# The corners of TensorE taken diagonally, and a gate on GpSimd taken away, in a linear-attention and SiLU feed-forward kernel

## The chip, the cores and the metric

The kernel runs on one core of a Trainium2 chip. A core has five engines, each with its own queue of instructions that it takes in order: TensorE (PE in the profile; its weight loads are PEld), VectorE (DVE), ScalarE (ACT), GpSimd (POOL) and SyncE (SP), which here only issues transfers. The engines wait for each other through semaphores. The metric is the device time of one execution in microseconds (us), the median of several runs.

## The reference: what is computed

q, k and v have 8 batches, 8 heads, 576 positions and 64 features in float32. For each batch and head:

```
q_s = softmax of q over its 64 features
k_s = softmax of k over the 576 positions
kv  = k_s^T v                (64 x 64)
attn = q_s kv                (576 x 64)
x = attn, heads side by side (4608 tokens x 512)
h = x w_in                   (4608 x 2048)
out = (h * sigmoid(h)) w_out (4608 x 512)
```

## The kernel before

**Tiling.** The 4608 tokens are taken in 9 chunks of 512 (`TCH`), the attention in 8 batches of 576. For each chunk t the kernel forms x, multiplies by w_in (the "group" products, `group`, line 374), applies SiLU, and multiplies by w_out (`prod`, line 474). Both large products are done by a scheme with seven block products in place of eight (products 1 to 7, taken in the order 1, 2, 6, 5, 7, 4, 3). It needs sums and differences of blocks as operands. For the second product these are S1, S2, S3 and S4, made by `s_op` on VectorE from the SiLU's output: S2 is made from S1, S4 from S2. Product 5 reads S1, product 6 reads S2, product 7 what S3 wrote, product 3 reads S4.

**Attention.** Two heads share the 128 partitions in places: TensorE's array of 128 x 128 is used as four corners of 64 x 64. A corner has a row half (the 64 partitions of its operands) and a column half (the 64 partitions of its output). `kv(b, cc)` (line 195) makes k^T v of four heads with 9 steps j of four products each, one for every corner, with 65 columns (64 of v and one that sums k's weights). There r is the row half and PS's bank, s the column half. `xt_mm` (line 234) makes x^T: four products, one for each corner, with s the row half and the bank and r the column half. `vaug` is the bfloat16 copy of v with the extra column, made by `vcast`, in two halves cc = 0 and 1, on GpSimd for batches 2 to 7. `qnorm` (GpSimd, line 163) multiplies exp(q) by the reciprocal of its sum, which VectorE makes (lines 154 and 158). `q_transpose` (SyncE) then transposes it by a transfer.

**Order.** The program is written out by hand. A list `units` holds TensorE's work in units of eight products, from chunk 1 on alternately of chunk t's group products and of chunk t-1's second products (`four_pairs`). `plan(u, f)` puts other work in front of unit u; whatever it issues goes into the queue of its engine at that place of the program. `full(t)` plans chunks 2 to 6. There u is the chunk's first unit and b = t + 1 the batch whose attention is prepared. Every queue runs in its own order, and an instruction starts as soon as its semaphores allow.

**Around the change.** For chunk 2 alone the second half of batch 3's v is treated differently. Batch 3's loads are issued late, by SyncE in front of the group products of chunk 1's last third (q 0, k 1, k 0, v 0, v 1, q 1, in this order). `vcast_at` puts in front of that cast a copy of one element of S2 into the tile `gate` on GpSimd. GpSimd, which works in order, so starts the cast only when S2 has been made. It is planned at unit 6 of chunk 2, S1 at unit 4 and S2 at unit 5. The PS banks that matter: a chunk's group products 5, 3 and 2 are gathered in banks 2 and 3, and `group_add` (line 352, VectorE) reads them, so that TensorE's next product 2 or 5 must wait for that addition. In the last chunk S1 and S2 are made in two halves: `plan(begin[NCH] - 11, ...)` gives S1's second half.

Of the kernel before, what the change touches and what calls it, by code (L numbers as in the profile page):

```python
# [17 lines left out]
def kernel(  # L18
# [9 lines left out]
    nc = tc.nc  # L28
# [12 lines left out]
    NCH = NT // TCH  # L41
# [21 lines left out]
    SS = {i: glob.tile([128, HF, HT], FP16, name=f"S{i}") for i in (1, 2, 4)}  # L63
# [8 lines left out]
    gate = glob.tile([1, 1], FP32, name="gate")  # L72
# [14 lines left out]
    def copy(eng, o, i):  # L87
        if eng is nc.scalar:
            eng.copy(out=o, in_=i)  # L89
        else:  # L90
            eng.tensor_copy(o, i)  # L91
# [7 lines left out]
    def jgd(b, name, cc):  # L99
        return st[b][name, cc].rearrange("p g (j d) -> p j g d", d=D)  # L100
# [4 lines left out]
    def exp_q(b, cc, g0=0, g1=2):  # L105
        if "eq" not in st[b]:
            st[b]["eq"] = ap.tile([128, J, NG * D], BF16, name="eq")
        nc.scalar.activation(  # L108
            out=half(st[b]["eq"], cc)[:, :, g0:g1], in_=jgd(b, "qt", cc)[:, :, g0:g1], func=ACT.Exp
        )  # L110

    def exp_k(b, cc):
        nc.scalar.activation(out=half(ek, cc), in_=jgd(b, "kt", cc), func=ACT.Exp)  # L113

    def vcast(b, cc, eng, g0=0, g1=2):
        o = vaug[:, :, 2 * cc + g0:2 * cc + g1, 0:D]
        i = jgd(b, "vt", cc)[:, :, g0:g1, :]
        copy(eng, o, i)

    def vcast_at(t, b, cc):  # L120

        if t == 2 and cc == 1:
            nc.gpsimd.tensor_copy(gate, SS[2][0:1, 0, 0:1])
        vcast(b, cc, nc.gpsimd)

    def qsum_pair(b, cc):
        e = half(st[b]["eq"], cc)
        t1 = mp.tile([128, 2 * TCH], FP32, name="h0", bufs=1)[:, 0:J * D]
        t1 = t1.rearrange("p (j g d) -> p j g d", g=2, d=D // 2)
        t2 = mp.tile([128, 2 * TCH], FP32, name=f"h{cc + 1}", bufs=1)[:, 0:J * D // 2]  # L130
        t2 = t2.rearrange("p (j g d) -> p j g d", g=2, d=D // 4)
        nc.gpsimd.tensor_tensor(  # L132
            out=t1, in0=e[:, :, :, 0:D // 2], in1=e[:, :, :, D // 2:D], op=ALU.add
        )
        nc.gpsimd.tensor_tensor(
            out=t2, in0=t1[:, :, :, 0:D // 4], in1=t1[:, :, :, D // 4:D // 2], op=ALU.add
        )
        st[b]["t2", cc] = t2
# [51 lines left out]

    def kv(b, cc):
        for j in range(J):
            for r in range(2):
                for s in range(2):
                    nc.tensor.matmul(  # L195
                        out=PS[s * 64:(s + 1) * 64, 6 + r, cc * 128:cc * 128 + E1],
                        lhsT=ek[r * 64:(r + 1) * 64, j, (2 * cc + s) * D:(2 * cc + s + 1) * D],
                        rhs=vaug[r * 64:(r + 1) * 64, j, 2 * cc + s, :],
                        start=(j == 0),
                        stop=(j == J - 1),  # L200
                    )
# [13 lines left out]
    def kv_both(b):  # L215
        kv(b, 0)
        kv(b, 1)
        kvcopy(b)
# [9 lines left out]
        return got  # L228

    def xt_mm(b, cc, col, n, bank, dst):  # L230
        for r in range(2):
            for s in range(2):
                h = slice(s * 64, (s + 1) * 64)
                nc.tensor.matmul(  # L234
                    out=PS[r * 64:(r + 1) * 64, bank + s, dst:dst + n],
                    lhsT=kvn[b % 3][h, cc, r, :],
                    rhs=st[b]["qT"][h, col // P:(col + n) // P, cc, r * 64:(r + 1) * 64],
                )
# [117 lines left out]
    def group_silu(t, i, f, n):  # L356
        x = group_bank(t, False) if i is None else four(t, i)
        nc.scalar.activation(out=group_out(t, f, n), in_=x, func=ACT.Silu, scale=1.0 / XS)  # L358

    def group(t, g, i, on=None, defer=False):  # L360
        bank = 0 if i in (1, 6, 7, 4) else 6 if t == 1 else 2
        w, f0, f1 = WS[g], 4 * g + 8, 4 * g
        a, bb = {
            1: (wa(0, f0), xb(t, 0, 0)),
            2: (wa(1, f0), xb(t, 1, 0)),
            3: (w[3], xb(t, 1, 1)),
            4: (wa(1, f1), XS4[3]),
            5: (w[0], XS4[0]),
            6: (w[1], XS4[1]),
            7: (w[2], XS4[2]),  # L370
        }[i]
        for p in range(4):
            for c in range(2):
                nc.tensor.matmul(  # L374
                    out=PS[:, bank + p // 2, (p % 2) * HT:(p % 2) * HT + width(t)],
                    lhsT=a[:, c, p * 128:(p + 1) * 128],
                    rhs=bb[:, c, 0:width(t)],
                    start=(i in (1, 2, 5) and c == 0 and p % 2 == 0),
                    stop=(i in (2, 3, 4) and c == 1 and p % 2 == 1),
                    skip_group_check=True,  # L380
                )
        on = on or {}
        if i == 1:
            group_snap(t, 0)
        elif i == 2:
            group_add(t, 0)
        elif i == 6:
            group_snap(t, 1, on.get(1, nc.scalar))
        elif i == 7:
            group_snap(t, 2, on.get(2, nc.scalar))  # L390
            group_add(t, 2)
        elif i == 4:
            group_silu(t, None, f1, 0)
        elif i == 3:
            if not defer:
                group_silu(t, 2, f1, 1)
                group_silu(t, 0, f0, 0)
            group_add(t, 1)
# [37 lines left out]
    def blk(t, kh, th):  # L436
        return GTS[t % 2][:, kh * HF:(kh + 1) * HF, th * HT:(th + 1) * HT]

    def s_op(t, i, f0=0, f1=HF):
        in0, in1, op = {  # L440
            1: (blk(t, 0, 1), blk(t, 1, 1), ALU.add),
            2: (SS[1], blk(t, 0, 0), ALU.subtract),
            3: (blk(t, 0, 0), blk(t, 0, 1), ALU.subtract),
            4: (blk(t, 1, 0), SS[2], ALU.subtract),
        }[i]
        f = slice(f0, f1)
        o = blk(t, 0, 1) if i == 3 else SS[i]
        nc.vector.tensor_tensor(out=o[:, f], in0=in0[:, f], in1=in1[:, f], op=op)
# [170 lines left out]
    def plan(u, f):  # L619
        at.setdefault(u, []).append(f)  # L620
# [7 lines left out]
    begin = {1: len(units)}  # L628
# [3 lines left out]
    def b_units(t, order):  # L632
        got = []
        for i in order:
            got.append(lambda t=t, i=i: prod(t, i, 0))

            def second(t=t, i=i):
                prod(t, i, 1)
                after(t, i)

            got.append(second)
        return got
# [11 lines left out]
    def full(t):  # L654
        begin[t] = u = len(units)
        b = t + 1
        bs = b_units(t - 1, ORDER)
        gs = [
            lambda g=g, i=i: group(t, g, i, {1: nc.vector} if g else {2: nc.vector}, True)
            for g in (1, 0)  # L660
            for i in ORDER
        ]
        for x in 2 * four_pairs:
            units.append({"b": bs, "g": gs}[x].pop(0))
        for i, x in ((1, 4), (2, 5), (3, 15), (4, 19)):
            plan(u + x, lambda i=i: s_op(t - 1, i))
        for g, at3 in ((1, (13, 17, 15)), (0, (23, 28, 25))):
            f1, f0 = 4 * g, 4 * g + 8
            for i, x, f, n in zip(range(3), at3, (f0, f0, f1), (0, 1, 1)):
                plan(u + x, lambda i=i, f=f, n=n: group_silu(t, i, f, n))  # L670
        more = b + 1 < B
        for i in range(2):
            plan(u + (3, 10)[i], lambda i=i: exp_q(b, i))
            plan(u + (7, 11)[i], lambda i=i: qsum(b, i))
            plan(u + (16, 17)[i], lambda i=i: qnorm(b, i, nc.gpsimd))
            plan(u + (2, 6 if t == 2 else 11)[i], lambda i=i: vcast_at(t, b, i))
            plan(u + (6, 4)[i], lambda i=i: exp_k(b, i))
            if more:
                plan(u + (5, 12)[i], lambda i=i: load(b + 1, "qt", q, i, nc.sync))
                plan(u + (8, 6)[i], lambda i=i: load(b + 1, "kt", k, i, nc.sync))  # L680
                plan(u + (22, 23)[i], lambda i=i: load(b + 1, "vt", v, i, nc.sync))
        plan(u + 17, lambda: q_transpose(b))
        plan(u + 15, lambda: kv_both(b))
        plan(u + 22, lambda: xt(t + 1, 0, nc.vector))
        plan(u + 27, lambda: xt(t + 1, 1))
        plan(u, lambda: (xs_op(t, 1), xs_op(t, 2), xs_op(t, 3), xs_op(t, 4)))
# [24 lines left out]

    begin[NCH] = len(units)
    last = NCH - 1
    plan(begin[NCH] - 11, lambda: s_op(last, 1, 4, 8))
    plan(begin[NCH] - 7, lambda: s_op(last, 2, 4, 8))
    plan(begin[NCH], lambda: (s_op(last, 1, 0, 4), s_op(last, 2, 0, 4), s_op(last, 3)))
    plan(begin[NCH] + 6, lambda: s_op(last, 4))
# [139 lines left out]
```

## Time and profile before

| what | us |
|---|---|
| median of 3 runs | 262.11 (262.06 to 262.53) |
| the profiled execution | 262.06 |
| its span | 260.3 |
| TensorE busy | 251.4 |
| VectorE busy | 206.8 |
| ScalarE busy | 187.6 |
| GpSimd busy | 66.3 |

The span runs from the first to the last instruction on the core; the profiled execution's own time is 1.8 us longer than its span. The lines quoted below are of two kinds. A line of the timeline gives the start and the length in us, the engine, the line of the kernel, the operation, what it writes and reads (`out<-in`), the shape and how many instructions were merged; in brackets stands how long the engine stood idle before it, and what ended that. TensorE's products are pipelined: the time of a merged group of eight includes the tail of the last, so the distance from one group's start to the next, 0.87 us, is the true pace. The lines on transfers give the time from issue to landing. PS is the memory that TensorE writes, W the weights, GT the SiLU's output, S any of S1, S2 and S4, T the differences of w_out's blocks (T1 to T4), XT and XS x^T and its differences, h the sums between the group products, WS differences of w_in's blocks.

### The profile page before, as it was taken

The numbers are of one execution on the slowest core, as the hardware profiler recorded it, in microseconds if no ns is written. First come the engines' busy times: TensorE is split into PE (matmuls) and PEld (weight loads), VectorE is DVE, ScalarE is ACT, GpSimd is POOL, SyncE is SP. The second block draws the span as 40 slices with busy tenths as digits, with TensorE's granted clock in tenths as the row PEclk, the third lists the DMA queues.
The fourth block names the chain that finished last, engine by engine and source line by source line (L and its number), as shares of the span: only waits on it lengthen the run. The fifth ranks groups of instructions, "written<-read, shape, count | busy, mean of one in ns | idle before, by whom it ended". The sixth has DMA issues, their size and how long they took to land.

```text
span 260.3 us, 6411 instructions
## 1 busy us (share of the span) xinstructions
PE 251.4 (97%) x2732; PEld 203.0 (78%) x2732; DVE 206.8 (79%) x268; ACT 187.6 (72%) x212; POOL 66.3 (25%) x63
## 2 busy tenths in 40 slices
PE   8799999999999999999999999999999999999992
PEld 3357756656888888888888888888888888888881
DVE  2957798888997999799979997999798548855832
ACT  5757887898993899489948994899473848484610
POOL 1753791640351205030502060306000000000003
PEclk9999999999999999999999999999999999999999
DMA  7999999689989485958694869630443004300624
GB/s 256 342 193 299 303 329 331 237 181 390 306 306 254 108 248 189 240 119 223 213 256 107 229 209 193 166 75 3 91 87 77 3 0 88 76 3 1 141 63 121
DMA packets 35452, 45.89 MB, mean 176 GB/s; under 512 B 16208, under 2 KB 19984, under 8 KB 35424
## 3 DMA queue, kind: packets, MB, share of 16 engines
q1 hardware_dynamic: 29568, 33.69, 47.6%
q0 software_dynamic: 5616, 11.60, 16.9%
q8 instruction: 21, 0.34, 0.5%
q10 hardware_dynamic: 240, 0.20, 0.2%
q14 instruction: 7, 0.06, 0.1%
HBM read 36.70 MB, written 9.44 MB: 177 GB/s over the span
## 4 chain that ended last, share of the span: by engine, by line
PE 88%; DVE 4%; ACT 2%; POOL 2%; DMA 1%; issue 1%; POOLq 0%; ACTq 0%
PE PS L474 37%; PE PS L374 35%; PE PS L411 5%; PE PS L264 3%; PE PS L282 2%; PE PS L234 2%; PE PS L195 2%; DMA qt<-in_q_dram 1%; DVE eq L163 1%; DVE zq L154 1%; ACT sg L256 1%; POOL out_dram L736 1%; ACT eq L108 1%; DVE GT L257 1%; POOL h L132 0%
## 5 line engine op out<-in xcount | busy, mean ns | idle before, releaser
L352 DVE TENSOR_TENSOR h<-PS,h 128x1024 f32<-128x1024 f32 (+1 forms) x45 | 54.0, 1199 | 13.0 <-ACT h L89 6.8
L474 PEld LDWEIGHTS <-GT 128*128 128x128 f16 x512 | 49.5, 98 | 6.9 <-issue 1.2
L374 PEld LDWEIGHTS <-WS 128*128 128x128 f16 x480 | 46.8, 98 | 6.4 <-issue 0.4
L474 PE MATMUL PS<-W,GT 128*128 128x256 f16 x384 | 49.1, 273 | 0.0
L374 PE MATMUL PS<-XS,WS 128*128 128x256 f16 (+1 forms) x360 | 46.3, 272 | 0.0
L358 ACT ACTIVATE GT<-h 128x1024 f16<-128x1024 f32 (+1 forms) x45 | 46.1, 1047 | 0.3 <-DVE h L352 0.3
L89 ACT COPY h<-PS 128x1024 f32<-128x1024 f32 (+1 forms) x35 | 35.1, 1003 | 13.4 <-PE PS L374 12.9
L163 POOL TENSOR_TENSOR eq<-eq,rzq 128x1152 bf16<-128x1152 bf16 x13 | 27.7, 2133 | 53.8 <-DVE rzq L158 53.4
L474 PEld LDWEIGHTS <-S 128*128 128x128 f16 x384 | 37.2, 98 | 5.2 <-issue 1.0
L374 PEld LDWEIGHTS <-W 128*128 128x128 f16 x360 | 34.7, 98 | 4.8 <-issue 0.5
L474 PE MATMUL PS<-T,S 128*128 128x256 f16 x256 | 32.7, 273 | 0.0
L374 PE MATMUL PS<-XT,W 128*128 128x256 f16 (+1 forms) x240 | 29.5, 272 | 0.1
L358 ACT ACTIVATE GT<-PS 128x1024 f16<-128x1024 f32 (+1 forms) x15 | 15.2, 1016 | 18.9 <-PE PS L374 18.9
L91 POOL CAST vaug<-vt 128x1152 bf16<-128x1152 f32 x12 | 14.8, 1239 | 43.3 <-DMA vt<-in_v_dram 43.3
L736 POOL DMA_DIRECT2D out_dram<-ow x5 | 2.7, 546 | 72.5 <-DVE ow L721 72.5
L108 ACT ACTIVATE eq<-qt 128x1152 bf16<-128x1152 f32 (+1 forms) x18 | 19.0, 1057 | 2.5 <-DMA qt<-in_q_dram 2.5
L154 DVE TENSOR_REDUCE zq<-eq 128x18 f32<-128x1152 bf16 x12 | 16.1, 1346 | 3.8 <-ACT eq L108 3.8
L113 ACT ACTIVATE ek<-kt 128x1152 bf16<-128x1152 f32 x16 | 18.3, 1153 | 0.8 <-DMA kt<-in_k_dram 0.8
L264 PE MATMUL PS<-XT,W 128*128 128x288 f16 x128 | 16.4, 286 | 0.5 <-DVE XT L91 0.2
L474 PE MATMUL PS<-W,S 128*128 128x256 f16 x128 | 16.5, 273 | 0.0
L494 DVE SCALAR_TENSOR_TENSOR ow<-PS,sc 128x512 f32<-128x512 f32 x7 | 4.8, 692 | 14.5 <-ACT sc L490 14.5
L264 PEld LDWEIGHTS <-W 128*128 128x128 f16 x128 | 12.4, 98 | 4.4 <-issue 1.3
(79 smaller groups left out, 345.4 us busy)
## 6 DMA issues: line engine op xcount, KB each, us to landing
out_dram<-ow SPq DMA_DIRECT2D x64, 128.0 KB, 2.4
qt<-in_q_dram SPq DMA_DIRECT2D x12, 576.0 KB, 4.7
kt<-in_k_dram SPq DMA_DIRECT2D x12, 576.0 KB, 5.7
vt<-in_v_dram SPq DMA_DIRECT2D x12, 576.0 KB, 5.4
qt<-in_q_dram POOLq DMA_DIRECT2D x4, 576.0 KB, 10.5
kt<-in_k_dram POOLq DMA_DIRECT2D x4, 576.0 KB, 13.9
vt<-in_v_dram POOLq DMA_DIRECT2D x4, 576.0 KB, 12.9
W<-in_moe_w_out_dram POOLq DMA_DIRECT2D x4, 512.0 KB, 15.0
```

The lines of the kernel that those rows point to most:

```text
L89: eng.copy(out=o, in_=i)
L91: eng.tensor_copy(o, i)
L108: nc.scalar.activation(out=half(st[b]["eq"], cc)[:, :, g0:g1], in_=jgd(b, "qt", cc)[:, :, g0:g1], func=ACT.Exp)
L113: nc.scalar.activation(out=half(ek, cc), in_=jgd(b, "kt", cc), func=ACT.Exp)
L154: nc.vector.reduce_sum(out=z, in_=e, axis=AX.X)
L163: eng.tensor_tensor(out=e, in0=e, in1=r[:, :, :, None].to_broadcast([128, J, 2, D]), op=ALU.mult)
L264: nc.tensor.matmul(out=PS[:, 2 * (fb % 3) + n, 0:S // 2], lhsT=W1[:, c, fb * 128:(fb + 1) * 128], rhs=XTS[0][:, c, n * (S // 2):(n + 1) * ...
L352: nc.vector.tensor_tensor(out=four(t, i), in0=group_bank(t, True), in1=four(t, i), op=ALU.add)
L358: nc.scalar.activation(out=group_out(t, f, n), in_=x, func=ACT.Silu, scale=1.0 / XS)
L374: nc.tensor.matmul(out=PS[:, bank + p // 2, (p % 2) * HT:(p % 2) * HT + width(t)], lhsT=a[:, c, p * 128:(p + 1) * 128], rhs=bb[:, c, 0:wid ...
L411: nc.tensor.matmul(out=PS[:, 2 + tb, :], lhsT=GTS[t % 2][:, fc, tb * 128:(tb + 1) * 128], rhs=W2[:, fc, :], start=(fc == 0), stop=(fc == N ...
L474: nc.tensor.matmul(out=PS[:, bank, m * HN:(m + 1) * HN], lhsT=a[:, fc, m * 128:(m + 1) * 128], rhs=bb[:, fc, :], start=(first and fc == 0) ...
```

## The change

Three edits:

- In `kv` and `xt_mm` the four corners are visited diagonally: first the two with r = s, then the two with r != s. Before, r was the outer loop and s the inner one.
- `vcast_at`, with the gate copy, is gone. Chunk 2's second cast is planned at unit 11, as in the other chunks, and has no gate.
- The second half of the last chunk's S1 is planned 9 units, not 11, before the end of the last chunk's units.

```
-    def vcast_at(t, b, cc):
-
-        if t == 2 and cc == 1:
-            nc.gpsimd.tensor_copy(gate, SS[2][0:1, 0, 0:1])
-        vcast(b, cc, nc.gpsimd)
-
...
     def kv(b, cc):
         for j in range(J):
-            for r in range(2):
-                for s in range(2):
+            for i in range(2):
+                for r in range(2):
+                    s = r ^ i
                     nc.tensor.matmul(
                         out=PS[s * 64:(s + 1) * 64, 6 + r, cc * 128:cc * 128 + E1],
...
     def xt_mm(b, cc, col, n, bank, dst):
-        for r in range(2):
-            for s in range(2):
+        for i in range(2):
+            for r in range(2):
+                s = r ^ i
                 h = slice(s * 64, (s + 1) * 64)
...
-            plan(u + (2, 6 if t == 2 else 11)[i], lambda i=i: vcast_at(t, b, i))
+            plan(u + (2, 11)[i], lambda i=i: vcast(b, i, nc.gpsimd))
...
-    plan(begin[NCH] - 11, lambda: s_op(last, 1, 4, 8))
+    plan(begin[NCH] - 9, lambda: s_op(last, 1, 4, 8))
```

## The prediction

> **What bounds the kernel now.** I read the page first, for the engine that carries the time and for the chain that ended last:
>
> ```profile
> PE 251.4 (97%) x2732; PEld 203.0 (78%) x2732; DVE 206.8 (79%) x268; ACT 187.6 (72%) x212; POOL 66.3 (25%) x63
> PE 88%; DVE 4%; ACT 2%; POOL 2%; DMA 1%; issue 1%; POOLq 0%; ACTq 0%
> ```
>
> PE fills 97% of the span and 88% of the chain. The granted clock is 1.00 in every stretch, so clock is no part of this case. From 62 us to 254 us PE's units of eight products start 0.873 us apart with hardly a break: what PE loses there, the kernel loses. So the question of each edit is whether PE starts a unit later or sooner. Then the timeline of PE, in chunk 2 and, in the last line, near the end of chunk 6:
>
> ```profile
> 69.68 1.04 PE L474 MATMUL PS<-T,S 128*128 128x256 f16 x8
> 75.01 0.81 PE L195 MATMUL PS<-vaug,ek 64*64 64x65 bf16 x72
> 79.26 1.04 PE L374 MATMUL PS<-XS,WS 128*128 128x256 f16 x8
> 186.72 0.41 PE L234 MATMUL PS<-qT,kvn 64*64 64x448 bf16 x8
> ```
>
> The reader is to see the first product that needs S2 (69.68), the group product 5 that needs PS bank 2 back (79.26), and how short the blocks of 64x64 corners are. Next VectorE in the same stretch, and one earlier line of the same kind of work:
>
> ```profile
> 51.19 1.85 DVE L458 TENSOR_TENSOR T<-W,T 128x2048 f16<-128x2048 f16 x1
> 66.66 1.22 DVE L448 TENSOR_TENSOR S<-GT 128x2048 f16<-128x2048 f16 x1
> 67.90 1.22 DVE L448 TENSOR_TENSOR S<-S,GT 128x2048 f16<-128x2048 f16 x1
> 69.05 1.34 DVE L154 TENSOR_REDUCE zq<-eq 128x18 f32<-128x1152 bf16 x1
> 74.99 2.35 DVE L448 TENSOR_TENSOR GT<-GT 128x2048 f16<-128x2048 f16 x1
> 77.87 1.22 DVE L352 TENSOR_TENSOR h<-PS,h 128x1024 f32<-128x1024 f32 x1
> ```
>
> S1 is the line at 66.66, S2 the next, S3 the one at 74.99: the same shape, but twice as long. Why shows in GpSimd's timeline:
>
> ```profile
> 49.84 2.12 POOL L163 TENSOR_TENSOR eq<-eq,rzq 128x1152 bf16<-128x1152 bf16 x1 [0.19 <-DVE rzq L158]
> 51.90 3.25 POOL L91 CAST vaug<-vt 128x1152 bf16<-128x1152 f32 x2
> 64.47 1.16 POOL L91 CAST vaug<-vt 128x1152 bf16<-128x1152 f32 x1 [9.31 <-DMA vt<-in_v_dram]
> 69.19 0.18 POOL L123 CAST gate<-S 1x1 f32<-1x1 f16 x1 [3.57 <-DMA out_dram<-ow]
> 69.32 1.15 POOL L91 CAST vaug<-vt 128x1152 bf16<-128x1152 f32 x1
> 74.14 2.12 POOL L163 TENSOR_TENSOR eq<-eq,rzq 128x1152 bf16<-128x1152 bf16 x1 [1.12 <-DVE rzq L158]
> ```
>
> GpSimd's qnorm holds from 74.14 to 76.26, and S3 ends at 77.34, 1.08 us after it: S3 stood still until qnorm was done. The same at 51.19: T2 waits for the qnorm that ends at 51.96 and ends 1.08 us later, and the two casts that GpSimd starts at 51.90 take 3.25 us instead of 2 x 1.15, because the first stands behind T2. So these two-input f16 operations of VectorE and GpSimd's casts and multiplies exclude each other, and the one that is later waits for the whole of the other. The casts at 64.47 and 69.32 lie beside a copy out of PS and a reduction, which keep their usual lengths: those do not exclude. Last, when the second v half of batch 3 is there:
>
> ```profile
> 56.58 1.11 SPq L97 DMA_DIRECT2D vt<-in_v_dram  x2
> DMA to landing us min/median/max: 7.7/8.4/9.1
> ```
>
> The first of the two is issued at 56.58 and lands 7.7 us later, at 64.28; its cast starts at 64.47, 0.19 later. The second is issued at 57.26 and takes 9.1 us: it lands at 66.36.
>
> **The change part by part.**
>
> *The gate goes.* GpSimd loses one 0.18 us copy, and its order is otherwise the same (cast 0, cast 1, qnorm 0, qnorm 1), so moving the cast's place in the plan from unit 6 to unit 11 moves nothing on its queue. But the second cast now waits only for its data: 66.36 + 0.19 = 66.55, not 69.32. It runs to 66.55 + 1.15 = 67.70, and S1, which VectorE reaches at 66.66, falls inside. S1 ends 1.08 after the cast: 68.78 instead of 66.66 + 1.22 = 67.88, so 0.9 us late. VectorE has no gap above 0.1 us from 66.66 to 80.2 (S2, reduction, reciprocal, addition, output, reduction, reciprocal, addition, S3, k-v copies, addition 77.87, S4), so the 0.9 goes through the whole queue. GpSimd's qnorms follow the reciprocals, so the qnorm that holds S3 comes 0.9 later too and gives nothing back. Whether PE feels it:
> - S2's end goes from 69.13 to 70.03. A waiting PE starts about 0.05 us after VectorE's end (the addition that ends at 241.03 lets the unit at 241.08 go). PE wanted S2 for the unit at 69.68, and its weight load 0.11 before. It starts at about 70.09: PE is 0.41 late.
> - The unit at 72.30 waits for the addition that ends at 71.84; this becomes 72.74 + 0.05 = 72.79, against 72.71: PE is 0.49 late. The units at 73.17 and 75.75 have margins of 0.74 and 0.68, enough for the difference.
> - The unit at 79.26 overwrites bank 2, which the addition of 77.87 to 79.08 reads. Its margin is 0.18 - 0.05 = 0.13 us. With 0.9 the addition ends at 79.98, and the unit starts at 80.03: PE is 0.77 late. This wait ends last and sets the sum.
> Behind it VectorE idles from 80.2 to 81.83 until ScalarE brings a snapshot that follows PE, and catches up. Nothing later gives the 0.77 back: PE's one wait for VectorE after that (0.2 us at 241.08) follows PE's own products.
>
> Also moved by the 0.9: SyncE's transposed copy of q, which waits for qnorm 1, from 76.28 to 77.2. It takes 4.6 us to land, 81.8, against x's products at 81.97 + 0.77. Behind it on SyncE are batch 4's v loads, which land at about 83.8 and 86.5 and are wanted at 101.2, and stores that wait for VectorE anyway. Hidden, by 0.9 us at the least. In the other chunks no cast was gated, so nothing changes.
>
> *The gate's own 0.18 us* gains nothing: GpSimd's next work, qnorm 0 at 70.90, waits for VectorE's reciprocal, not for GpSimd.
>
> *S1's first half of the last chunk, two units later in the plan.* No VectorE instruction is issued in those two units; VectorE's order is the same before and after. Zero, at both ends.
>
> *The corners.* The k-v blocks are 576/72 = 8 blocks' worth; each has 18 sets of four corners. 0.81 us less the last product's own 0.19 is 0.62 us, 34 ns a set. A product of 65 columns at the rate of the large ones (0.873 us for 8 x 256 columns, 0.43 ns a column) streams 28 ns. So all four already run together. Best end: every set at 28 ns, 18 x 6 = 0.11 us a block, 0.9 us in all, if VectorE kept up (its margin in the bank-2 unit is 0.13 a chunk). Worst end: corners that now overlap run in pairs; one more 28 ns a set gives 0.5 a block, 4.0 us in all, and x's products, 512 columns a set, 0.22 us in each of 18 sets, 4.0 more. I take zero: the old order has same-row neighbours in the k-v products (00, 01) and same-column neighbours in x's products, the new order swaps the two kinds, and both rows show four together: x's eight of 448 and 64 columns need 0.41 us, of which 512 x 0.43 = 0.22 is streaming.
>
> One more row on the corners: the eight weight loads of x's block at 186.71 are all done within 0.14 us, while the first four products still stream, in the same row groups as well as in others. [...]
>
> **Sum.** The profiled execution took 262.06 us (span 260.3 and 1.8 around it), 0.05 below the median of 262.11. 262.06 + 0.77 + 0 + 0 = 262.83; on the median's scale 262.88.
>
> **The rivals.**
> - *The data is early or half early.* The delay of VectorE is the landing less 65.47 (66.36 less 0.9). With the landing at 65.8, for instance, it is 0.33, S2 is in time and only the bank-2 unit loses 0.33 - 0.13 = 0.2: 262.3. For it: the other half's load needed 1.4 us less. Against: loads of one queue in a fixed order, and the same traffic before it.
> - *VectorE gets there first and keeps its turn* (the one on the other side). S1 truly starts when the copy before it ends, about 66.74. If the cast started after that, 0.2 us later than I have it, and S2 then followed without letting the cast in, the cast would run at 69.1 as now and cost nothing: 262.1. For it: 0.2 us is little. Against: T2's line at 51.19 shows the waiting cast going as soon as T2 ends; then S2 would be held instead, ending at 67.88 + 1.15 + 1.08 = 70.11, a delay of 0.98 and 262.95.
> - *The corners gain.* At the best end 0.9, less what chunk 2 does not pass on (its end is set by VectorE): 262.1 with the cast's cost, 261.4 without.
> - *The corners pair up*: 4 to 8 us, 267 to 271.
>
> **How the numbers follow.** Forecast 0.65, early data 0.10, VectorE first 0.10, corners gain 0.10, corners pair up 0.05. The likeliest gives 262.88, with 262.6 to 263.1 as its own range (delay of 0.65 to 0.98, and noise). The range of 262.0 to 263.2 holds the first three and part of the fourth. What a measurement of this kernel can tell from no change is about 0.2%, 0.52 us. Slower by more: the forecast (0.61 of 0.65) and pairs, 0.66. Within: early data, VectorE first, half the corners' gain, the forecast's rest, 0.27. Faster: 0.07.
>
> **What would show it.** In the changed kernel's profile: GpSimd's second cast near 66.55 and 1.15 long; S1 about 2.1 us instead of 1.22; S2's end near 70.0; PE's unit at 69.68 near 70.1 and that at 79.26 near 80.03; all later units 0.77 late; L195 blocks still 0.81 and L234's 448-column one 0.41. Wrong if S1 stays at 1.22, if the cast starts after 67.9, or if a corner block changes by more than 0.05 us.

## The result, and the profile after

| what | before | after |
|---|---|---|
| median, us | 262.16 (262.06 to 262.53, 4 runs) | 263.38 (263.28 to 263.65, 4 runs) |
| the profiled execution | 262.06 | 263.28 |
| its span | 260.3 | 261.5 |

The change costs 1.22 us: the ratio is 1.0046, with a 95% interval of 1.0028 to 1.0063. The prediction was 262.88, so the direction is right, and the loss of 1.22 us is 0.45 larger than the 0.77 forecast; 263.38 lies above the upper end of 263.2. The start-up of the profiled executions varies by up to 0.36 us, so the text below says where a lateness holds a part of that.

The profile's page of the changed kernel, first the busy times, then the chain that ended last:

```profile
PE 251.8 (96%) x2732; PEld 203.1 (78%) x2732; DVE 208.0 (80%) x268; ACT 187.5 (72%) x212; POOL 65.6 (25%) x62
PE 82%; DVE 7%; DMA 4%; ACT 2%; POOL 2%; issue 1%; SPq 1%; POOLq 0%; DVEq 0%; ACTq 0%
```

TensorE (PE) carries 82% of the chain in place of 88%, VectorE 7% in place of 4%. (The 4% of DMA are a load of v at 3.36 us, long before the change.) Most of VectorE's new share lies in one place. Followed backwards, the chain leaves TensorE at 80.49 us and returns to it only at 65.8. These are pieces of it in order of time (start, length, what):

```profile
65.80 0.02 issue
65.82 1.23 DVE h L91
67.04 1.82 DVE S L444
...
68.89 1.23 DVE S L444
...
74.98 1.08 DVE h L348
76.06 2.63 DVE GT L444
...
79.22 1.23 DVE h L348
80.44 0.04 issue
80.49 1.03 PE PS L370 x8
```

So in chunk 2 the whole queue of VectorE, from S1 to the addition that frees PS bank 2, became the path. TensorE's units in the same stretch (timeline; start and length):

```profile
70.17 1.05 PE L470 MATMUL PS<-T,S 128*128 128x256 f16 x8
72.88 1.03 PE L370 MATMUL PS<-XT,WS 128*128 128x256 f16 x8
75.59 0.80 PE L190 MATMUL PS<-vaug,ek 64*64 64x65 bf16 x72
80.49 1.03 PE L370 MATMUL PS<-XS,WS 128*128 128x256 f16 x8 [0.49 <-DVE h L348]
187.94 0.41 PE L230 MATMUL PS<-qT,kvn 64*64 64x448 bf16 x8
```

The S2 unit is 0.49 late (69.68 before), the unit of 72.30 is 0.58 late, the bank-2 unit of 79.26 is 1.23 late, and every later unit, to the last product, keeps that (187.94 against 186.72). The two corner blocks keep their length to 0.01 us. VectorE and then GpSimd show why:

```profile
66.96 1.90 DVE L444 TENSOR_TENSOR S<-GT 128x2048 f16<-128x2048 f16 x1
68.89 1.23 DVE L444 TENSOR_TENSOR S<-S,GT 128x2048 f16<-128x2048 f16 x1
74.72 0.27 DVE L152 RECIPROCAL rzq<-zq 128x18 f32<-128x18 f32 x1
75.98 2.71 DVE L444 TENSOR_TENSOR GT<-GT 128x2048 f16<-128x2048 f16 x1
```

```profile
64.19 1.16 POOL L91 CAST vaug<-vt 128x1152 bf16<-128x1152 f32 x1 [8.73 <-PE PS L370]
66.63 1.16 POOL L91 CAST vaug<-vt 128x1152 bf16<-128x1152 f32 x1 [1.27 <-DMA vt<-in_v_dram]
71.89 2.12 POOL L157 TENSOR_TENSOR eq<-eq,rzq 128x1152 bf16<-128x1152 bf16 x1 [4.10 <-DVE rzq L152]
75.49 2.12 POOL L157 TENSOR_TENSOR eq<-eq,rzq 128x1152 bf16<-128x1152 bf16 x1 [1.49 <-ACT GT L354]
```

S1 is held by the cast, as forecast: the cast ends at 67.79, S1 1.07 later. But S3, too, is longer: 2.71 us instead of 2.35. It starts 0.99 late and ends 1.35 late. The reciprocal that qnorm 1 (GpSimd's line at 75.49) waits for ends at 74.99 (74.72 and 0.27). The trace's record of GpSimd's wait stands at 75.016, and qnorm 1 starts 0.474 us after it. Before, the same record stood at 74.031 and qnorm 1 started 0.106 after it. S3 ends 1.08 after qnorm 1 in both kernels. Nothing that the prediction named delays it there: GpSimd had stood idle for 1.49 us. The profile names ScalarE as the releaser; the experiments show below that this is not it.

One more difference has no part in the change: in this execution the first loads landed later (v's first half, for instance, 0.7 us later), so that TensorE was some 0.3 late already at 14 us, and S1, by the timelines, starts 0.30 late. Of the 1.23 at the bank-2 unit, 0.93 was lost in chunk 2. In the same way S3's start is 0.99 late, of which the meeting of S1 and the cast made 0.68.

### The profile page after: what moved, and what is told of

Same layout as the page of the kernel before. It is cut to its first block, busy times and chain, and to the rows that moved or that the text cites. A ratio compares the mean times of both kernels' runs of the same rounds, so it can differ in the third digit from the quotient of the medians.

```text
span 261.5 us, 6410 instructions
## 1 busy us (share of the span) xinstructions
PE 251.8 (96%) x2732; PEld 203.1 (78%) x2732; DVE 208.0 (80%) x268; ACT 187.5 (72%) x212; POOL 65.6 (25%) x62
## 4 chain that ended last, share of the span: by engine, by line
PE 82%; DVE 7%; DMA 4%; ACT 2%; POOL 2%; issue 1%; SPq 1%; POOLq 0%; DVEq 0%; ACTq 0%
PE PS L470 34%; PE PS L370 33%; PE PS L407 5%; DMA vt<-in_v_dram 4%; PE PS L260 3%; PE PS L278 2%; PE PS L230 2%; PE PS L190 2%; DVE h L348 1%; DVE S L444 1%; DVE GT L444 1%; DVE zq L148 1%; SPq L97 1%; POOL out_dram L732 1%; ACT sg L252 1%
```

## The experiments

The theory after this first profile: the gate's removal is the whole loss, through S1 held by the cast, and the corners and S1's move are free. The first rival: part of the loss is the corners'. Unless another base is named, the short diffs are against the kernel before. In the last chunk "S1's half" and "S2's half" are elements 4 to 8 of `s_op`, made first; the texts call them the first or the second half.

**The corners and S1's move alone, with the gate kept** (the loop's edit stands in `kv` and in `xt_mm`; it is shown once).

```
-            for r in range(2):
-                for s in range(2):
+            for i in range(2):
+                for r in range(2):
+                    s = r ^ i
...
-    plan(begin[NCH] - 11, lambda: s_op(last, 1, 4, 8))
+    plan(begin[NCH] - 9, lambda: s_op(last, 1, 4, 8))
```

> The kernel before with the diagonal corners and the last chunk's S1 half two units later, and with the gate kept. Theory (the gate is the cause): no change, 262.2 us within 0.2; the k-v blocks keep 0.59 us from first to last start, S1 in chunk 2 keeps 1.22 us. Rival (the corners cost something where the start-up waits for its loads, as the changed kernel's first 14 us were 0.31 us late): 0.3 us slower, 262.5, with the loss in the first 14 us.

Measured: 262.23 against 262.16, ratio 1.0003 (0.9994 to 1.0012). The last product starts at 254.937 us, before at 254.94. The k-v block of chunk 2 and x's block near 186.7, from this kernel's timeline:

```profile
75.03 0.80 PE L196 MATMUL PS<-vaug,ek 64*64 64x65 bf16 x72
```

```profile
186.71 0.41 PE L236 MATMUL PS<-qT,kvn 64*64 64x448 bf16 x8
```

Before they took 0.81 and 0.41. The order of the corners and the place of S1's half are worth nothing that this kernel can show.

**The gate alone taken away, with the old corners.**

```
-            plan(u + (2, 6 if t == 2 else 11)[i], lambda i=i: vcast_at(t, b, i))
+            plan(u + (2, 11)[i], lambda i=i: vcast(b, i, nc.gpsimd))
```

> The kernel before with the gate taken away and nothing else. Theory: chunk 2's second cast meets S1, S1 takes 1.9 to 2.1 us and the unit that overwrites bank 2 is 0.8 to 0.95 us late: 263.0 to 263.1. Rival (the corners carry part of the loss): the same in chunk 2 but 0.3 less in all than the changed kernel, with a start-up like that of before in every profile.

Measured: 263.26, ratio 1.0039 (1.0027 to 1.0051). This one edit has the whole loss, as far as the two intervals can tell (1.0028 to 1.0063 for the full change). But the meeting went the other way round here. In this kernel's timelines of VectorE and GpSimd:

```profile
66.75 1.22 DVE L448 TENSOR_TENSOR S<-GT 128x2048 f16<-128x2048 f16 x1
68.00 2.06 DVE L448 TENSOR_TENSOR S<-S,GT 128x2048 f16<-128x2048 f16 x1
```

```profile
66.86 2.12 POOL L91 CAST vaug<-vt 128x1152 bf16<-128x1152 f32 x1 [1.30 <-DMA vt<-in_v_dram]
```

The cast came 0.11 us after S1, waited for it, went as soon as S1 ended, and then held S2 (2.06 us instead of 1.22). VectorE loses about as much as when S1 is held: with the start-up taken off (S1 starts 0.09 late here), S3 starts 0.83 late, against 0.68 in the changed kernel's first execution. And qnorm 1 again starts late after its wait (0.463 us), so S3 takes 2.70.

**The changed kernel again.**

> The changed kernel once more. Theory: the 0.31 us that its profiled execution lost before 14 us is chance in the landing of the first loads, so this profile shows another figure there, while chunk 2 loses 0.92 us again; median 263.1 to 263.4. Rival: both losses come back with the same sizes, 263.4.

Measured: 263.51, ratio 1.0057 (1.0036 to 1.0077). Here the start-up is as before (S1 starts 0.01 earlier), so the 0.3 of the first profile belongs to that execution and not to the kernel. VectorE got there first again (S1 at 66.64, cast at 66.97 and 1.92 long, S2 2.06 long), qnorm 1 is late by the same amount (0.479 after its wait), and the bank-2 unit 1.08 late, nearly all of it lost in chunk 2.

**v's loads ahead.** To take the meeting away without a gate, batch 3's loads go in another order, so that both casts run long before S1. The base is the changed kernel.

```
-        ("qt", q, 0), ("kt", k, 1), ("kt", k, 0), ("vt", v, 0), ("vt", v, 1), ("qt", q, 1)
+        ("qt", q, 0), ("kt", k, 1), ("vt", v, 0), ("vt", v, 1), ("kt", k, 0), ("qt", q, 1)
```

> The changed kernel, without the gate, but with batch 3's loads in the order q 0, k 1, v 0, v 1, k 0, q 1, so that v 1 lands at about 64.3 us in place of 66.4 and k 0 at about 66.4 (wanted at 67.9). Theory: the second cast runs from about 64.5 to 65.7, ahead of S1, S1 takes 1.22 us and nothing is lost in chunk 2: 262.1 to 262.2, as the kernel before, without any gate. Rival (the missing gate costs in another way than by meeting S1): the loss of 0.9 stays.

Measured: 262.53, ratio 1.0012 (1.0002 to 1.0022). The expectation is missed: most of the loss is gone, but not all. GpSimd's timeline of this kernel, and VectorE's S3:

```profile
62.79 1.25 POOL L91 CAST vaug<-vt 128x1152 bf16<-128x1152 f32 x1 [7.56 <-DMA vt<-in_v_dram]
64.30 1.16 POOL L91 CAST vaug<-vt 128x1152 bf16<-128x1152 f32 x1 [0.26 <-DMA vt<-in_v_dram]
70.97 2.12 POOL L157 TENSOR_TENSOR eq<-eq,rzq 128x1152 bf16<-128x1152 bf16 x1 [5.51 <-DVE rzq L152]
74.56 2.12 POOL L157 TENSOR_TENSOR eq<-eq,rzq 128x1152 bf16<-128x1152 bf16 x1 [1.47 <-DVE rzq L152]
```

```profile
73.80 0.27 DVE L152 RECIPROCAL rzq<-zq 128x18 f32<-128x18 f32 x1
75.06 2.70 DVE L444 TENSOR_TENSOR GT<-GT 128x2048 f16<-128x2048 f16 x1
```

The casts meet nothing, S1 and S2 have their 1.22, S3 starts nearly in time (75.06 against 74.99), and yet qnorm 1 starts 0.459 after its wait, so S3 is held 0.35 longer. This is a second cost, apart from the meeting. Two explanations were open. A: the number of GpSimd instructions ahead of qnorm 1 decides; the gate's copy is gone, so there is one fewer. B: the casts ran early and left GpSimd idle for 5 us and more, and a GpSimd that was idle starts late.

**A copy that holds nothing, in the gate's place** (v's loads ahead, as above; the plan's units as in the changed kernel).

```
     def vcast_at(t, b, cc):
         if t == 2 and cc == 1:
-            nc.gpsimd.tensor_copy(gate, SS[2][0:1, 0, 0:1])
+            nc.gpsimd.tensor_copy(gate, st[b]["vt", cc][0:1, 0, 0:1])
```

> The changed kernel with v loaded ahead of k 0, as in the run before, and with a copy of one element on GpSimd in the place of the old gate that waits for nothing but v (it holds nothing back). In the run without it, GpSimd's qnorm 1 of batch 3 started 0.46 us after its last semaphore in place of 0.11. Theory A (the number of GpSimd's instructions ahead of qnorm 1 decides, one fewer puts a stop of 0.35 us in front of it): qnorm 1 starts 0.11 after the semaphore, the bank-2 unit is in time, 262.2. Theory B (the stop comes from casts that ran early, leaving GpSimd idle for 5 us and more): the 0.46 stays, 262.5.

Measured: 262.19, ratio 1.0000 (0.9992 to 1.0009). qnorm 1 starts 0.107 after its wait, and S3 takes 2.35, though GpSimd stood idle for 5.43 us before qnorm 0. The loss is gone.

**The same with the extra instruction some 25 us earlier:** the changed kernel with v's loads ahead, and one element set by GpSimd behind batch 2's v loads. The expectation puts it at about 42 us; in the trace it runs at 39.65.

```
-    plan(b1 + 6, lambda: (load(2, "vt", v, 0, nc.gpsimd), load(2, "vt", v, 1, nc.gpsimd)))
+    plan(b1 + 6, lambda: (load(2, "vt", v, 0, nc.gpsimd), load(2, "vt", v, 1, nc.gpsimd), nc.gpsimd.memset(gate, 0.0)))
```

> As the last one, but the one additional GpSimd instruction is a memset of one element at about 42 us, thirty us earlier, behind the transfers that GpSimd issues. Theory A: the count ahead of qnorm 1 is that of the kernel before, so qnorm 1 starts 0.11 after its semaphore, 262.2. Theory B: 0.46 and 262.5.

Measured: 262.10, ratio 0.9995 (0.9987 to 1.0004). GpSimd's timeline of this kernel has nearly the same idle time ahead of qnorm 0 as the one that was late (5.80 against 5.51 us), and from qnorm 0's end to qnorm 1's wait both have 1.01. Yet qnorm 1 is in time, 0.106 after its wait:

```profile
63.88 1.16 POOL L91 CAST vaug<-vt 128x1152 bf16<-128x1152 f32 x1 [0.31 <-DMA vt<-in_v_dram]
70.84 2.12 POOL L157 TENSOR_TENSOR eq<-eq,rzq 128x1152 bf16<-128x1152 bf16 x1 [5.80 <-DVE rzq L152]
74.08 2.12 POOL L157 TENSOR_TENSOR eq<-eq,rzq 128x1152 bf16<-128x1152 bf16 x1 [1.12 <-DVE rzq L152]
```

B falls: the idle time is no shorter, and the count differs.

**The changed kernel with the extra instruction and its own loads,** that is, the meeting without the late qnorm. The edit is that of the copy that holds nothing, with batch 3's loads in their old order.

> The changed kernel with the loads in its own order and the same additional copy that holds nothing back. The cast still meets S1 or S2. Theory A: the late qnorm is gone, so only the meeting is left: S2 0.9 to 1.0 us late, the bank-2 unit 0.75 to 0.9 late, 262.9 to 263.0, which is what the prediction had. Theory B: as the changed kernel, 263.3 to 263.4.

Measured: 262.93, ratio 1.0028 (1.0018 to 1.0039). VectorE's timeline of this kernel:

```profile
66.61 2.26 DVE L449 TENSOR_TENSOR S<-GT 128x2048 f16<-128x2048 f16 x1
68.90 1.23 DVE L449 TENSOR_TENSOR S<-S,GT 128x2048 f16<-128x2048 f16 x1
```

The cast runs from 66.634 for 1.149, S1 ends 1.08 after it, and S3 has its usual 2.345. The bank-2 unit is 0.87 late, 0.92 with the start-up taken off. This is the case that the prediction described, within 0.05 us of its 262.88; in this execution the meeting cost VectorE 1.04 us, a little more than the 0.9 forecast.

**One GpSimd instruction fewer in the kernel before,** with gate, loads and order kept: the 128x128 memset under the identity, in the first microsecond, goes to VectorE.

```
-    make_identity(nc, ident_f)
+    nc.vector.memset(ident_f, 0.0)
+    make_identity(nc, ident_f, nomemset=True)
```

> The kernel before with its gate and its loads, and one GpSimd instruction fewer at the very start: the 128x128 memset ahead of the identity goes to VectorE. Nothing is moved at chunk 2; only the number of GpSimd instructions ahead of qnorm 1 falls by one. Theory A (the number of GpSimd instructions ahead of qnorm 1 decides whether it stops): qnorm 1 of chunk 2 starts 0.46 us after its semaphore in place of 0.11, S3 behind it takes 2.70 in place of 2.35, the unit of output bank 2 comes 0.2 to 0.3 later than start-up accounts for, and the kernel takes 262.4 to 262.5, as with v's loads early and no filler (262.53). Rival: only an instruction taken away beside the casts, or the early casts themselves, bring the stop, and one fewer at the start changes nothing: 0.11, 2.35, 262.16.

Measured: 262.57 against 262.24, ratio 1.0014 (1.0005 to 1.0023). VectorE's reciprocal and S3, then GpSimd's timeline:

```profile
73.94 0.27 DVE L158 RECIPROCAL rzq<-zq 128x18 f32<-128x18 f32 x1
75.20 2.70 DVE L448 TENSOR_TENSOR GT<-GT 128x2048 f16<-128x2048 f16 x1
```

```profile
69.53 1.15 POOL L91 CAST vaug<-vt 128x1152 bf16<-128x1152 f32 x1
71.11 2.12 POOL L163 TENSOR_TENSOR eq<-eq,rzq 128x1152 bf16<-128x1152 bf16 x1 [0.43 <-issue]
74.70 2.12 POOL L163 TENSOR_TENSOR eq<-eq,rzq 128x1152 bf16<-128x1152 bf16 x1 [1.47 <-DVE rzq L158]
```

An instruction taken away seventy us earlier makes qnorm 1 late (0.459 after its wait), holds S3 0.35 longer and puts the bank-2 unit 0.44 late, of which 0.21 came from the start. Theory A holds in both directions at this place: one fewer brings the late start, one more takes it away. ScalarE, which the profile names in the changed kernel, is not the cause: here and with v's loads ahead VectorE's reciprocal ended the wait, and the start is as late.

**A wait near the end, apart from the change.** In the kernel before, TensorE waits 0.2 us at 241.08 for an addition that stands behind S2's half. The half goes two units later.

```
-    plan(begin[NCH] - 7, lambda: s_op(last, 2, 4, 8))
+    plan(begin[NCH] - 5, lambda: s_op(last, 2, 4, 8))
```

> The kernel before with the first half of the last chunk's S2 planned two units later, so that VectorE makes the addition at 239.81 us ahead of it. Theory (PE's one late wait, 0.2 us at 241.08, is for this addition, which stood behind that half of S2): the addition ends 0.6 earlier, the wait at 241.08 is gone, and the end is 0.2 us sooner, 261.9 to 262.0. Rival: S2's half is then late for the end of the last chunk and nothing is won, 262.2.

Measured: 261.95 against 262.16, ratio 0.9991 (0.9983 to 1.0). The unit starts at 240.93, and the addition comes ahead of S2's half in this kernel's timeline:

```profile
239.13 1.22 DVE L352 TENSOR_TENSOR h<-PS,h 128x1024 f32<-128x1024 f32 x1
240.26 0.68 DVE L448 TENSOR_TENSOR S<-S,GT 128x1024 f16<-128x1024 f16 x1
```

**The three edits together:** the changed kernel with v's loads ahead, the early extra instruction and S2's half later (three edits shown above).

> The changed kernel with v's loads of the last batch ahead, the one-element GpSimd memset at 42 us, and the second half of S2 of the last chunk planned two units later (the addition at 239.8 goes ahead of it). The two gains were measured apart: 262.10 against 262.16, and 261.95 against 262.16. If they add: 261.88, ratio 0.9989, with the unit that was at 241.08 coming 0.2 us earlier against start-up. If the later half is covered by the earlier one: 261.95.

Measured: 261.98 against 262.24, ratio 0.9991 (0.9982 to 1.0). The two small gains do not add. The traces show why: with the start-up taken off, the last product starts 0.21 us earlier with S2's half later, 0.01 earlier with the early extra instruction, and 0.21 earlier with all three. The 262.10 was no gain of its own. Both intervals reach 1, so even the 0.2 us is within what this kernel's measurement can tell from no change.

## Why the prediction was right and wrong

- *S1 starts in the second cast's time and ends 1.08 us after it.* Right in the first execution (cast at 66.63, S1's end 1.07 after the cast's) and in the changed kernel with the extra instruction. In the two other runs of an ungated second cast VectorE was first, and S2 was held instead. The prediction had this order as a rival, and its "against" said that S2 would then be held and the delay be 0.98. That is what happened, with 0.83: coming first does not save VectorE. Which of the two comes first changed between two executions of the same kernel: the cast starts between 66.63 and 66.97 in the four runs, S1 between 66.61 and 66.96.
- *VectorE's 0.9 goes through the queue.* Right: what S1 and S2 lose together arrives at S3's start. With the start-up taken off, S3 starts 0.68, 0.83, 0.84 and 1.04 late in the four runs with the meeting, around the 0.9 forecast.
- *The S2 unit 0.41 late, the unit at 72.30 0.49 late.* With the start-up taken off they are 0.35 and 0.43 late in the changed kernel's second execution, 0.19 and 0.28 in the first, 0.55 and 0.63 with the extra instruction. Right in kind; the size follows the meeting's.
- *"GpSimd loses one 0.18 us copy, and its order is otherwise the same", and the qnorm that holds S3 "comes 0.9 later too and gives nothing back".* This is the step that failed: the prediction let qnorm 1 follow its reciprocal as promptly as before. The order is the same, but the count is not: with one instruction fewer ahead of it, qnorm 1 starts 0.46 to 0.48 us after its wait instead of 0.106. So it comes later than the reciprocal does by another 0.35 to 0.37 us, and S3's end with it. Why the count matters stays open.
- *The bank-2 unit sets the sum, with a margin of 0.13.* Right as a rule, wrong in what went into it. The table takes S3's start and end and the bank-2 unit from the traces, each against the kernel before (74.990, 77.335 and 79.256 us). S1's start (66.655 before) stands for the start-up, which these figures hold:

| kernel | S1 starts late | S3 starts late | S3 ends late | bank-2 unit late | difference of the last two |
|---|---|---|---|---|---|
| changed, first execution | 0.304 | 0.986 | 1.351 | 1.232 | 0.119 |
| changed, again | -0.010 | 0.828 | 1.201 | 1.078 | 0.123 |
| gate alone taken away | 0.092 | 0.921 | 1.277 | 1.155 | 0.122 |
| changed, with the extra instruction | -0.049 | 0.990 | 0.990 | 0.867 | 0.123 |
| changed, v's loads ahead | 0.074 | 0.070 | 0.422 | 0.299 | 0.123 |
| before, one instruction fewer | 0.216 | 0.212 | 0.564 | 0.443 | 0.121 |

The last column is the margin: 0.12 us in every row. So the sum's formula holds in six executions of five kernels. The term that the prediction put at nothing is the step from S3's start to its end, 0.35 to 0.37 us in the five rows without the instruction, and 0 with it. All of it reaches TensorE where VectorE is late anyway. With the start-up taken off, the 0.77 of the prediction's sum becomes 0.93, 1.09 and 1.06 in the first three rows. The first of these is no larger than the 0.92 with the extra instruction, because there the meeting itself cost less (0.68 against 1.04); S3's own length tells the two losses apart. In time, the changed kernel took 263.38 and 263.51, and 262.93 with the extra instruction.
- *The corners and S1's half at zero.* Right: ratio 1.0003 with both, blocks within 0.01 us. The bounds of 0.9 us gained and 8 us lost were far wider than needed; the rows that showed four corners running together gave the right value.
- *The gate's own 0.18 us gains nothing.* Right, and incomplete: its absence costs some 0.35 us of VectorE's time.

The range was too narrow because its bounds took in when the cast's data lands, and nothing about when an instruction starts that has its data.

## What to carry to other kernels

A gate that looks like a lost wait may keep two engines' operations apart; here, without it, the one of S1 and S2 that met the cast took 1.90 to 2.26 us in place of 1.22. Before a gate goes, look whether the freed work falls on the other engine's critical operation, and expect the loss whichever comes first: here VectorE lost 0.68 and 1.04 us with the cast first, 0.83 and 0.84 with S1 first. Moving the transfer earlier avoided the meeting here without a gate: S1 and S2 took 1.22 and 1.23 us. When a queue gains or loses an instruction, compare the time from the record of a wait to the start of the instruction behind it, in both traces, and not the order alone. If an instruction that everything waits for starts late after its wait, one cheap instruction more, ahead of it on that engine, is worth a try: here it brought 0.459 us down to 0.106 at 39.65 us and to 0.107 beside the casts.

## What the runs showed of the hardware

- **At one place of this program, GpSimd's start after a wait depended on how many instructions came before.** It was 0.106 or 0.107 us with the gate's copy or with either instruction in its place, even one at 39.65 us; 0.459 to 0.479 with one fewer, in five executions of four kernels. Behind it, in the first trace of the changed kernel, the next three batches' qnorm 1 starts 0.109 us after its wait (at 101.56, 127.75 and 153.95), and every cast from batch 3 on 0.122 to 0.125 after its own; in the kernel before it is 0.109 or 0.110, and 0.122 to 0.124 for all casts but the gated one. Counting the records of GpSimd in the trace from zero, waits included, the late qnorm 1 is number 68 in the changed kernel and in the kernel before with a memset fewer; in the kernel before and with the early extra instruction it is number 69, and number 68 is its wait. No view of these traces names what holds GpSimd there, and counts other than these two were not tried. In each of the twelve traces one packet of 8,192 bytes on an instruction queue (q14) begins near here, but 0.37 to 1.50 us after qnorm 1 has started, late or not; the late start did not wait for that packet.
- **Where VectorE's two-input f16 operations met GpSimd's casts and qnorms in these runs, one was held until the other ended, and turns alternated.** With the gate alone taken away, the cast behind S1 took 2.12 us instead of 1.16, then S2 behind the cast 2.06 instead of 1.22. The held VectorE operation (S1, S2, or S3 behind qnorm 1) ended 1.07 to 1.08 us after GpSimd's. The engine that waited went next, before the first one's following operation: that cast, waiting from 66.86, ended at 68.98, and S2, which VectorE began at 68.00, ended at 70.06.
